# Identity products that nobody reads, and another order of the first chunk's steps, in a fused mLSTM and GELU kernel

## The chip, the cores and the metric

The kernel runs on one core of a Trainium2 chip. The metric is the device time of one execution in microseconds (us). The core's engines work side by side, each through its own list of instructions in the order in which the program issued them: PE (TensorE, matrix products), DVE (VectorE, elementwise work), ACT (ScalarE, functions from tables and copies), POOL (GpSimd) and the queue that issues the transfers. A step that needs another engine's result waits on a semaphore.

## What is computed

An mLSTM cell runs over 768 positions for 4 batches of 8 heads of 40 elements. Its output, as 3072 rows of 320, goes through a layer with an exact GELU.

```python
# per position t; q, k, v, o: (B, H, D), i and f: (B, H); B, H, D = 4, 8, 40
m_new = maximum(f + m, i)
C = exp(f + m - m_new) * C + exp(i - m_new) * outer(v, k)
n = exp(f + m - m_new) * n + exp(i - m_new) * k
y = sigmoid(o) * (C @ q) / maximum(abs(n @ q), 1)
# then x = y as (3072, 320), w_in (320, 2048), w_out (2048, 320)
h = x @ w_in
out = (0.5 * h * (1 + erf(h / sqrt(2)))) @ w_out
```

The two weights come as 64-bit floats.

## The kernel before

The sequence is cut into six chunks of 128 positions, and each chunk into its four batches. For a chunk the cell becomes a handful of matrix products; the layer follows for the 512 rows of the chunk. The chunks after the first are computed in one dense pattern, in which the cell of the next chunk runs between the rows of the layer of this one. The first part, called the front, has more to do: it computes the gates, the cell of chunk 0, the cell of chunk 1, the layer of chunk 0, and it converts the weights from 64-bit to 32-bit floats on DVE and ACT, piece by piece.

The front is played from a list of words. A letter names a step, a digit its batch or piece:

```python
FRONT = """
    O0 L0 P0 g0 L2 E t0 P1 N P2 w0 K L1 D w1 Q P3 O2 s0 w2 t1 O1 c0 J v0 K t2 s1 L3 w3 g1 v1 O3 J y0 c1 K B5 y1 s2
    x0 O4 L4 t3 J x1 K B4 g2 L5 s3 v2 c2 g3 c3 y2 v3 G0 x2 J K A M1 y3 x3 L6 J M0 K H K O5 O7 J T0 J W0 O6 A S0 W1 K
    ...
"""
def play(order, steps):
    for word in order.split():
        if word[0] not in "AU":
            first_up()
        steps[word[0]](*[int(x) for x in word[1:].split(",") if x])
```

Small letters are steps of chunk 0 and capitals the same of chunk 1: m mask, w weights, g gate, t turn (transpose k and q), s scores, c carry (the state), v values, y finish, x turn y. E and N are the later gates, D and Q their transposed decays. L and O load q, k and v, o; P fetches a piece of the weights, B loads maxima; K and J are the two halves of a conversion, Z sums of weights; A and U are up-products (x times w_in, then GELU), F down-rows (times w_out).

The steps that the change touches, with cuts. The class is `Cell`, `c` the chunk and `b` the batch. Line numbers in the profile are those of this kernel: L360 is the transpose in `turn`, L381 the product in `scores`, L399 and L404 those in `carry`, L428 in `values`, L453 in `turn_y`; L521 and L527 are the up-products, L634 the down-rows of chunk 0.

```python
def weights(self, b):            # w: exp(a - M), from a broadcast M
    ...
            if h % 4 == 0:       # chunk 0 only
                pm = ps_mm.tile([P, 4, L], F32, name="pm", tag="b")
                for j in range(4):
                    nc.tensor.matmul(pm[:, j, :], row[...].to_broadcast([3 * BH, P]), M_parts, ...)
                nc.tensor.matmul(pm, eye, beyond..., ...)
    ...
def turn(self, b):               # t
    for src, store, name in ((kb, self.kT, "kT"), (qb, self.qT, "qT")):
        pt = ps_tr.tile([P, NP, L], F32, name="pt", tag="tr")
        for p in range(NP):
            nc.tensor.transpose(pt[:, p, :], src[n % NLD][...], ident)
        store[b] = two.tile([P, NP, L], F32, name=name, tag=name)
        nc.scalar.copy(out=store[b], in_=pt)
...
def scores(self, b):             # s
    ps = [pool.tile([P, NP, L], F32, name="ps", tag=tag) for hip in range(2)]
    for p in range(NP):
        for hip in range(2):
            r = halves[hip]
            nc.tensor.matmul(ps[hip][:, p, :], kT[r, p, :], qT[r, p, :], start=True, stop=True)
    for hip in range(2):
        nc.vector.tensor_tensor(out=w, in0=ps[hip], in1=w, op=OP.mult)      # w: half of W[n]

def carry(self, b):              # c
    pf = ps_h.tile([P, H + NP, D1], F32, name="pf", tag="h")
    pc = pf[:, H:H + NP, :]
    if c == 0:
        self.weigh_values(b)     # vw = v * exp(...), on DVE
    ...
            nc.tensor.matmul(pc[halves[hip], p, :], kb[n % NLD][...], vw[...], start=True, stop=True)
    ...
            if c == 0:
                nc.scalar.copy(out=st, in_=pc[r])
    ...
def values(self, b):             # v
    ph = pool.tile([P, H, D1], F32, name="ph", tag=tag)
    for h in range(H):
        for r in halves:
            nc.tensor.matmul(ph[r, h, :], Pm[:, h, r], vb[n % NLD][:, h, :], start=True, stop=True)
    ...
def turn_y(self, b):             # x
    ...
    for k in range(NX + 1):
        nc.tensor.transpose(px[:, k, :], ob[n % NLD][:, k * P:(k + 1) * P], ident)
    nc.scalar.copy(out=xT[:, :, t], in_=px)
```

`finish` (y) is six instructions on DVE, the first three of which read the result of `values`. `conv_one` (K) is an instruction on DVE, two on ACT that follow it, and two more on DVE; `conv_two` (J) is two on DVE, the first of which needs ACT's, and then the fetch of a later piece.

Of the kernel before, what the change touches and what calls it, by code (L numbers as in the profile page):

```python
# [15 lines left out]
P = 128  # L16
# [6 lines left out]


FRONT = """
    O0 L0 P0 g0 L2 E t0 P1 N P2 w0 K L1 D w1 Q P3 O2 s0 w2 t1 O1 c0 J v0 K t2 s1 L3 w3 g1 v1 O3 J y0 c1 K B5 y1 s2
    x0 O4 L4 t3 J x1 K B4 g2 L5 s3 v2 c2 g3 c3 y2 v3 G0 x2 J K A M1 y3 x3 L6 J M0 K H K O5 O7 J T0 J W0 O6 A S0 W1 K
    M2 J C0 T1 U U K K Z V0 J T2 L7 G1 A M3 W2 J W3 S1 C1 Z A K S2 K Z Y0 C2 J G2 J V1 T3 K K U U Y1 S3 Z C3 J V2 K
    J F F F K J K J Z Z K J K J F F G3 J K K X0 V3 F J F Z F F F J K J Y2 K K J X1 K F F J K J J F Z F X2 F B9 B8 Y3
    X3 F"""  # L30
DOWN = """
    M0 Z M1 T0 W0 F F T1 W1 Z G3 Z F S0 Z S1 C0 M2 Z C1 G1 G0 M3 V0 Y0 Z V1 W2 Z F F T2 W3 F T3 F G2 Z Y1 S2 S3 C2
    V2 C3 Y2 V3 F F Y3 X0 F F X1 X2 F F X3 F"""
# [3 lines left out]
def kernel(  # L37
# [16 lines left out]
    nc = tc.nc  # L54

    B, H, S, D = q.shape
    L = P
    NCH = S // L
# [36 lines left out]
    ident = const.tile([P, P], F32, name="ident")  # L95
# [114 lines left out]
    def decays_turned(e0, e1, g0, g1):  # L210
        e, g = slice(e0, e1), slice(g0, g1)
        gates_turned((ew[:, e], ewT[:, e]), (gg[:, g], gT[:, g]))
        pd = ps_tr.tile([P, g1 - g0, BH], F32, name="pd", tag="tr")
        nc.tensor.matmul(pd.rearrange("p c n -> p (c n)"), last, gT[:, g].rearrange("p c n -> p (c n)"),
                         start=True, stop=True)
        nc.vector.tensor_copy(out=dec[:, g], in_=pd)
# [88 lines left out]

    halves = (slice(0, R), slice(R, P))

    def per_head(t, c, b):
        return t[:, c, b * H:(b + 1) * H].unsqueeze(2)

    class Cell:
# [14 lines left out]
        def weights(self, b):  # L326

            n = self.c * B + b
            W[n] = wts.tile([P, H, L], F32, name="W", tag="W")
            if self.c > 0:  # L330
                M_n = Mb.pop(n)
            for h in range(H):
                r = b * H + h
                if self.c > 0:
                    src = M_n[:, h, :]
                else:


                    if h % 4 == 0:
                        pm = ps_mm.tile([P, 4, L], F32, name="pm", tag="b")  # L340
                        for j in range(4):
                            nc.tensor.matmul(pm[:, j, :], row[:, r + j:r + j + 1].to_broadcast([3 * BH, P]), M_parts,
                                             start=(j == 0), stop=False, skip_group_check=True)
                        nc.tensor.matmul(pm, eye, beyond.unsqueeze(1).to_broadcast([P, 4, L]), start=False, stop=True,
                                         skip_group_check=True)
                    src = pm[:, h % 4, :]
                nc.scalar.activation(out=W[n][:, h, :], in_=src, func=AF.Exp, scale=-1.0, bias=aT[:, self.c, r:r + 1])  # L347
            if self.c > 0 and not 2 * B <= n + NM < 2 * B + NM:
                load_M(n + NM)
# [5 lines left out]
        def turn(self, b):  # L355
            n = self.c * B + b
            for src, store, name in ((kb, self.kT, "kT"), (qb, self.qT, "qT")):
                pt = ps_tr.tile([P, NP, L], F32, name="pt", tag="tr")
                for p in range(NP):
                    nc.tensor.transpose(pt[:, p, :], src[n % NLD][:, 2 * p:2 * p + 2, :].rearrange("p h d -> p (h d)"),  # L360
                                        ident)
                store[b] = two.tile([P, NP, L], F32, name=name, tag=name)
                nc.scalar.copy(out=store[b], in_=pt)
            if 0 < self.c < NCH - 1:
                self.weigh_values(b)
# [6 lines left out]
        def scores(self, b):  # L372
            n = self.c * B + b
            kT, qT = self.kT.pop(b), self.qT[b]

            pool, tag = (ps_tr, "tr") if self.c > 0 and b % 2 else (ps_mm, "a")
            ps = [pool.tile([P, NP, L], F32, name="ps", tag=tag) for hip in range(2)]
            for p in range(NP):
                for hip in range(2):
                    r = halves[hip]  # L380
                    nc.tensor.matmul(ps[hip][:, p, :], kT[r, p, :], qT[r, p, :], start=True, stop=True)  # L381
            for hip in range(2):
                w = W[n].rearrange("p (m two) t -> p m two t", two=2)[:, :, hip, :]
                nc.vector.tensor_tensor(out=w, in0=ps[hip], in1=w, op=OP.mult)  # L384

        def carry(self, b):

            c, n = self.c, self.c * B + b
            qT = self.qT.pop(b)

            pf = ps_h.tile([P, H + NP, D1], F32, name="pf", tag="h")
            pc = pf[:, H:H + NP, :]
            if c == 0:
                self.weigh_values(b)
            if c + 1 < NCH:
                vw = self.vw.pop(b)
                for p in range(NP):
                    for hip in range(2):
                        nc.tensor.matmul(pc[halves[hip], p, :], kb[n % NLD][:, 2 * p + hip, :], vw[:, 2 * p + hip, :],  # L399
                                         start=True, stop=True)  # L400
            if c > 0:
                for p in range(NP):
                    for r in halves:
                        nc.tensor.matmul(pf[r, 2 * p:2 * p + 2, :].rearrange("p h d -> p (h d)"), qT[:, p, r],  # L404
                                         state[b][:, p, :], start=True, stop=True)
                self.far[b] = two.tile([P, H, D1], F32, name="far", tag="far")
                nc.vector.tensor_tensor(out=self.far[b], in0=pf[:, 0:H, :],
                                        in1=per_head(gT, c - 1, b).to_broadcast([P, H, D1]), op=OP.mult)
            if c + 1 < NCH:
                for hip in range(2):  # L410
                    r, m = halves[hip], slice(D1 * hip, D1 * hip + D1)
                    st = state[b][r, :, m]
                    if c == 0:
                        nc.scalar.copy(out=st, in_=pc[r])
                    else:
                        d = dec[r, c - 1, b * H:(b + 1) * H].rearrange("p (m two) -> p m two", two=2)[:, :, hip:hip + 1]
                        self.engine.tensor_tensor(out=st, in0=st, in1=d.to_broadcast([DP, NP, D1]), op=OP.mult)  # L417
                        nc.vector.tensor_tensor(out=st, in0=st, in1=pc[r], op=OP.add)

        def values(self, b):  # L420
            n = self.c * B + b
            Pm = W.pop(n)

            pool, tag = (ps_mm, "a") if self.c > 1 else (ps_h, "h")
            ph = pool.tile([P, H, D1], F32, name="ph", tag=tag)
            for h in range(H):
                for r in halves:
                    nc.tensor.matmul(ph[r, h, :], Pm[:, h, r], vb[n % NLD][:, h, :], start=True, stop=True)  # L428
            if self.c == 0:
                self.hs[b] = ph  # L430
                return
            hs = self.hs[b] = two.tile([P, H, D1], F32, name="hs", tag="hs")
            nc.vector.tensor_tensor(out=hs, in0=ph, in1=self.far.pop(b), op=OP.add)
# [12 lines left out]
        def turn_y(self, b):  # L446
            n, t = self.c * B + b, slice(b * L, (b + 1) * L)
            if self.c > 0:
                px = ps_tr.tile([P, NX + 1, L], F32, name="px", tag="tr")
            else:  # L450
                px = ps_mm.tile([P, NX + 1, L], F32, name="px", tag="b")
            for k in range(NX + 1):
                nc.tensor.transpose(px[:, k, :], ob[n % NLD][:, k * P:(k + 1) * P], ident)  # L453
            nc.scalar.copy(out=xT[:, :, t], in_=px)  # L454
            if self.c > 0:
                load(n + NLD)
            if self.c > 0 and b == B - 1:
                sum_x()
# [259 lines left out]
    def cell_steps(c, letters):  # L718
# [4 lines left out]
    first_g = Hidden(False)  # L723
    n_pieces = range(len(pieces))
    steps = dict(P=fetch, L=lambda n: load(n, 0, 2), O=lambda n: load(n, 2, 4), B=load_M, E=second_gates, N=later_gates,
                 D=lambda: decays_turned(0, 2, 0, 1), Q=lambda: decays_turned(2, NCH - 1, 1, NCH - 1),
                 A=in_turn(first_up_steps(0)), U=in_turn(first_up_steps(1)), F=in_turn(first_down_steps(first_g)),
                 K=in_turn(lambda i=i: conv_one(i) for i in n_pieces), H=sums_begin,
                 J=in_turn(lambda i=i: conv_two(i) for i in n_pieces), Z=in_turn(lambda i=i: in_sum(i) for i in range(8)))
# [46 lines left out]
```

## Time and profile before

| what | value |
|---|---|
| device time, median of 3 | 525.6 us (524.04 to 525.65) |
| span of the profiled execution | 523.9 us |
| PE busy | 503.9 us, 96% |
| DVE busy | 342.0 us, 65% |
| ACT busy | 257.7 us, 49% |
| POOL busy | 60.2 us, 11% |
| moved by DMA | 41.62 MB, mean 79 GB/s |

"Busy" is the time in which an engine has an instruction under way; for PE it does not tell how fast the instruction runs. The granted clock tells that in part: 1.00 is full speed, 0.50 half. A row of the order of time gives the start, the busy time, and in brackets how long the engine was idle before it and whose result ended that. PE instructions of one group overlap a little, so the sum of a group's durations is more than the time it takes.

### The profile page before, as it was taken

How to read it: one execution, taken by the hardware profiler on the slowest of the kernel's cores; microseconds unless marked ns; L12 is line 12 of the kernel's file. 1: busy time of each engine (PE TensorE's matmuls, PEld its weight loads, DVE VectorE, ACT ScalarE, POOL GpSimd, SP SyncE). 2: the span in 40 equal slices, each digit the busy share in tenths (PEclk: the TensorE clock that was granted, in tenths of full speed). 3: DMA queues.
4: the chain of work that ended last, by engine and by line, in shares of the span. 5: the costliest groups of instructions: out<-in, count | busy, mean ns of one | idle time of the engine just before them, and what ended most of it. 6: DMA issues, size and time to landing. Idle time of an engine off the chain costs nothing.

```text
span 523.9 us, 10898 instructions
## 1 busy us (share of the span) xinstructions
PE 503.9 (96%) x4436; PEld 447.9 (85%) x4436; DVE 342.0 (65%) x711; ACT 257.7 (49%) x524; POOL 60.2 (11%) x98
## 2 busy tenths in 40 slices
PE   3778999999999999999999999999999999999997
PEld 2667888877788999988999988999988999988997
DVE  7579669999757898357478356578356547256521
ACT  5785999764342980143881134682134583134200
POOL 3001010000200044000054000053100021000000
PEclk9988999999999999999999999999999999999999
DMA  9989823259900134900124920024940020000001
GB/s 171 166 192 196 210 78 78 73 147 202 199 15 1 60 103 66 178 10 1 41 89 76 167 47 0 27 98 79 155 61 0 1 82 3 26 25 2 1 0 51
DMA packets 111442, 41.62 MB, mean 79 GB/s; under 512 B 101184, under 2 KB 104416, under 8 KB 111392
## 3 DMA queue, kind: packets, MB, share of 16 engines
q1 hardware_dynamic: 111392, 40.92, 37.7%
q8 instruction: 35, 0.57, 0.4%
q14 instruction: 15, 0.12, 0.1%
HBM read 36.90 MB, written 4.01 MB: 78 GB/s over the span
## 4 chain that ended last, share of the span: by engine, by line
PE 93%; DVE 4%; ACT 2%; issue 0%; DMA 0%; DVEq 0%; ACTq 0%
PE po L657 29%; PE pu L587 24%; PE pu L612 7%; PE po L634 7%; PE pu L521 5%; PE ps L381 5%; PE ph L428 4%; PE pt L360 4%; PE pf L404 2%; PE pf L399 2%; PE px L453 2%; PE pu L527 1%; DVE W L384 1%; DVE M L194 1%; DMA f_sb<-in_f_gate_dram 0%
## 5 line engine op out<-in xcount | busy, mean ns | idle before, releaser
L657 PE MATMUL po<-w_out,g 128*128 128x160 f32 x640 | 91.5, 299 | 0.0
L657 PEld LDWEIGHTS po<-w_out,g 128*128 128x128 f32 x640 | 88.0, 190 | 0.3 <-issue 0.3
L587 PE MATMUL pu<-xT,w_in 128*128 128x256 f32 x240 | 63.1, 386 | 0.0
L619 DVE TENSOR_TENSOR g<-pu,g 128x512 f32<-128x512 f32 x60 | 39.6, 688 | 34.5 <-PE pu L612 33.8
L587 PEld LDWEIGHTS pu<-xT,w_in 128*128 128x128 f32 x240 | 44.1, 190 | 10.3 <-issue 5.0
L384 DVE TENSOR_TENSOR W<-ps,W 128x512 f32<-128x512 f32 x48 | 30.2, 684 | 31.1 <-ACT W L347 21.1
L454 ACT COPY xT<-px 128x384 f32<-128x384 f32 x24 | 11.1, 479 | 77.8 <-PE px L453 77.8
L347 ACT ACTIVATE W<-Mb,aT 128x128 f32<-128x128 f32 x160 | 48.9, 391 | 0.1
L620 ACT ACTIVATE g<-g 128x512 f32<-128x512 f32 x60 | 37.1, 630 | 22.1 <-DVE g L619 20.2
L657 PE MATMUL po<-w_sums,sums 128*128 128x160 f32 x320 | 47.3, 302 | 0.0
L617 ACT ACTIVATE g<-pu 128x512 f32<-128x512 f32 x20 | 11.9, 597 | 70.0 <-PE pu L612 70.0
L657 PEld LDWEIGHTS po<-w_sums,sums 128*128 128x128 f32 x320 | 44.0, 190 | 0.4
L323 POOL TENSOR_SCALAR_AFFINE_SELECT Mb<-Mb 128x1024 f32<-128x1024 f32 x20 | 22.3, 1123 | 189.8 <-DMA Mb<-M_d 189.6
L612 PE MATMUL pu<-xT,w_rest 64*128 64x256 f32 x320 | 40.0, 389 | 0.0
L670 DVE TENSOR_TENSOR o_sb<-po,o_sb 128x320 f32<-128x320 f32 (+1 forms) x27 | 12.5, 464 | 41.5 <-PE po L657 36.2
L587 PE MATMUL pu<-x_sums,in_sums 128*128 128x256 f32 x160 | 37.8, 379 | 0.0
L612 PEld LDWEIGHTS pu<-xT,w_rest 64*128 64x128 f32 x320 | 29.3, 186 | 9.3 <-issue 6.6
L634 PE MATMUL po<-w_out,g 128*128 128x320 f32 x128 | 35.5, 434 | 0.0
L587 PEld LDWEIGHTS pu<-x_sums,in_sums 128*128 128x128 f32 x160 | 30.4, 190 | 4.1
L634 PEld LDWEIGHTS po<-w_out,g 128*128 128x128 f32 x128 | 23.9, 190 | 9.4
L521 PE MATMUL pu<-xT,w_in 128*128 128x256 f32 x128 | 29.3, 385 | 0.5 <-DVE W L384 0.5
L417 POOL TENSOR_TENSOR state<-state,dec 64x164 f32<-64x164 f32 x24 | 11.1, 464 | 162.0 <-PE pf L404 158.2
(132 smaller groups left out, 872.2 us busy)
## 6 DMA issues: line engine op xcount, KB each, us to landing
Mb<-M_d SPq DMA_DIRECT2D x20, 512.0 KB, 3.9
bits<-in_moe_w_in_dram SPq DMA_DIRECT2D x20, 256.0 KB, 3.9
bits<-in_moe_w_out_dram SPq DMA_DIRECT2D x16, 320.0 KB, 3.3
vb<-in_v_dram SPq DMA_DIRECT2D x24, 160.0 KB, 4.7
ob<-in_o_gate_dram SPq DMA_DIRECT2D x24, 160.0 KB, 4.0
qb<-in_q_dram SPq DMA_DIRECT2D x24, 160.0 KB, 4.6
kb<-in_k_dram SPq DMA_DIRECT2D x24, 160.0 KB, 4.7
out_dram<-o_sb SPq DMA_DIRECT2D x24, 160.0 KB, 2.9
```

Source lines behind the costliest of these rows:

```text
L323: nc.gpsimd.affine_select(out=t, in_=t, compare_op=OP.is_ge, fill=1.0e30, base=0, pattern=[[0, H], [1, L]], channel_multiplier=-1)
L347: nc.scalar.activation(out=W[n][:, h, :], in_=src, func=AF.Exp, scale=-1.0, bias=aT[:, self.c, r:r + 1])
L360: nc.tensor.transpose(pt[:, p, :], src[n % NLD][:, 2 * p:2 * p + 2, :].rearrange("p h d -> p (h d)"), ident)
L381: nc.tensor.matmul(ps[hip][:, p, :], kT[r, p, :], qT[r, p, :], start=True, stop=True)
L384: nc.vector.tensor_tensor(out=w, in0=ps[hip], in1=w, op=OP.mult)
L521: nc.tensor.matmul(banks[-1][e][:, i - i0, :], w_in[:, x, e, i * P:(i + 1) * P], xT[:, x, t0:t1], start=(x == 0 and i == i0), stop=False, ...
L587: nc.tensor.matmul(to[:, j, :], lhs[:, (f0 + j) * P:(f0 + j + 1) * P], rhs, start=(first and j == 0), stop=(last and j == 1), skip_group_c ...
L612: nc.tensor.matmul(pair[e][:, j, :], w_rest[halves[e], (f0 + j) * P:(f0 + j + 1) * P], xT[halves[e], NX, HT * h:HT * (h + 1)], start=False ...
L619: nc.vector.tensor_tensor(out=blk[e][h], in0=x, in1=y, op=OP.add)
L620: nc.scalar.activation(out=blk[e][h], in_=blk[e][h], func=AF.Gelu)
L634: nc.tensor.matmul(po[b], g.t[:, f, b * L:(b + 1) * L], w_out[:, f, :], start=(f == 0), stop=(f == NF - 1))
L657: nc.tensor.matmul(bank[at][:, i, :], lhs(j, t), rhs(j), start=(first and i == 0 and j == 0), stop=(i == n - 1 and j == HF - 1), skip_grou ...
```

## The change

A step `I` sets a counter. Each of six places in which PE begins a tile of results reads the counter and issues that many products of the identity with itself into the tile, before the products that the step needs; these overwrite what the identity products left, so that nobody reads it. The counter is then zero. The purpose is in the name `keep_clock`: to give PE something to do where it would stand idle, so that its clock stays up. Besides, the words of the front stand in another order; the later parts have the order of before.

```diff
 FRONT = """
-    O0 L0 P0 g0 L2 E t0 P1 N P2 w0 K L1 D w1 Q P3 O2 s0 w2 t1 O1 c0 J v0 K t2 s1 L3 w3 g1 v1 O3 J y0 c1 K B5 y1 s2
-    x0 O4 L4 t3 J x1 K B4 g2 L5 s3 v2 c2 g3 c3 y2 v3 G0 x2 J K A M1 y3 x3 L6 J M0 K H K O5 O7 J T0 J W0 O6 A S0 W1 K
-    M2 J C0 T1 U U K K Z V0 J T2 L7 G1 A M3 W2 J W3 S1 C1 Z A K S2 K Z Y0 C2 J G2 J V1 T3 K K U U Y1 S3 Z C3 J V2 K
-    J F F F K J K J Z Z K J K J F F G3 J K K X0 V3 F J F Z F F F J K J Y2 K K J X1 K F F J K J J F Z F X2 F B9 B8 Y3
-    X3 F"""
+    O0 L0 P0 I3 g0 L2 P1 E I2 t0 N w0 L1 K P2 D w1 Q O2 s0 P3 w2 t1 O1 c0 J v0 K t2 s1 w3 L3 g1 v1 I3 O3 J y0 c1 K
+    B5 y1 s2 x0 O4 t3 L4 J x1 K B4 L5 g3 s3 I7 v2 g2 c2 c3 y2 G0 v3 x2 K J A L6 y3 M1 J x3 M0 K H K O7 O5 J T0 J W0
+    O6 A S0 K W1 M2 J C0 T1 U U K K Z V0 J T2 L7 A M3 W2 J G1 S1 C1 Z W3 A K K G2 S2 Y0 C2 Z J J K V1 T3 G3 K U U Y1
+    S3 Z C3 J V2 K F F F J Z K J J K K J Z K J F F J V3 K X0 K F J Z F J F F F K J K Y2 K J X1 K F F F J K J F J F Z
+    X2 B8 B9 Y3 X3 F"""
...
+    idle = [0]
+
+    def keep_clock(steps):
+
+        idle[0] = steps
+
+    def unread(bank):
+        for _ in range(idle[0]):
+            nc.tensor.matmul(bank, ident, ident, start=True, stop=True, skip_group_check=True)
+        idle[0] = 0
...
                 pt = ps_tr.tile([P, NP, L], F32, name="pt", tag="tr")
+                unread(pt[:, 0, :])
...
             pf = ps_h.tile([P, H + NP, D1], F32, name="pf", tag="h")
             pc = pf[:, H:H + NP, :]
+            unread(pf.rearrange("p h d -> p (h d)")[:, 0:P])
...
             ph = pool.tile([P, H, D1], F32, name="ph", tag=tag)
+            unread(ph.rearrange("p h d -> p (h d)")[:, 0:P])
```

The same call stands in `weights`, `scores` and `turn_y`, and `I=keep_clock` joins the table of steps.

More of the change, by code (lines that the diff above doesn't have):

```diff
@@ L340, in weights @@
                         pm = ps_mm.tile([P, 4, L], F32, name="pm", tag="b")
+                        unread(pm[:, 0, :])
                         for j in range(4):
@@ L377, in scores @@
             ps = [pool.tile([P, NP, L], F32, name="ps", tag=tag) for hip in range(2)]
+            unread(ps[0][:, 0, :])
             for p in range(NP):
@@ L451, in turn_y @@
                 px = ps_mm.tile([P, NX + 1, L], F32, name="px", tag="b")
+            unread(px[:, 0, :])
             for k in range(NX + 1):
@@ L725 @@
     steps = dict(P=fetch, L=lambda n: load(n, 0, 2), O=lambda n: load(n, 2, 4), B=load_M, E=second_gates, N=later_gates,
-                 D=lambda: decays_turned(0, 2, 0, 1), Q=lambda: decays_turned(2, NCH - 1, 1, NCH - 1),
+                 I=keep_clock, D=lambda: decays_turned(0, 2, 0, 1), Q=lambda: decays_turned(2, NCH - 1, 1, NCH - 1),
                  A=in_turn(first_up_steps(0)), U=in_turn(first_up_steps(1)), F=in_turn(first_down_steps(first_g)),
```

## The prediction

> **What bounds the kernel now.** I read the page first, for the engine that is full; then the busy time by stage, for where it is not; then the granted clock in windows of 3.41 us; then the order of time on PE, ACT and DVE around the places so found.
>
> The page, busy time of the engines and the forty slices of the span:
>
> ```profile
> PE 503.9 (96%) x4436; PEld 447.9 (85%) x4436; DVE 342.0 (65%) x711; ACT 257.7 (49%) x524; POOL 60.2 (11%) x98
> ...
> PEclk9988999999999999999999999999999999999999
> ```
>
> TensorE (PE) is busy for 96% of the span, and the clock dips only in slices 3 and 4 (26 to 52 us). Then the stages, cut where one limit gives way to another (columns: stretch and length in us, then busy us and instructions of PE, of its weight loads, DVE, ACT, POOL, then granted clock, DMA share, GB/s):
>
> ```profile
> 0.00:16.00 16.00, 5.50 (x27) 3.90 (x27) 13.05 (x39) 9.22 (x20) 4.56 (x26) 1.00 0.83 166
> 16.00:29.19 13.19, 12.79 (x130) 10.44 (x131) 5.39 (x12) 10.05 (x30) 0.00 (x0) 1.00 1.00 173
> 29.19:54.60 25.41, 19.98 (x241) 17.19 (x240) 24.55 (x56) 17.16 (x36) 2.66 (x2) 0.87 0.97 195
> 54.60:62.30 7.70, 7.25 (x80) 6.06 (x78) 3.84 (x7) 7.59 (x16) 0.00 (x0) 1.00 0.96 217
> 62.30:137.70 75.40, 75.40 (x572) 59.72 (x573) 65.38 (x165) 55.63 (x102) 2.34 (x2) 1.00 0.53 123
> ```
>
> To 16 us DVE computes the gates (13.05 of 16); to 29 PE is the fuller; from 29.19 to 54.6 DVE never waits and PE has 5.4 us of holes; then ACT (7.59 of 7.70); from 62.3 on PE is full, and the table of waits has none of PE after 62.3. So every us by which the dense stretch starts sooner is a us of the total, and a us inside the DVE-bound stretch is worth nothing unless PE itself set the pace there.
>
> The clock in 29.19 to 54.6, same columns:
>
> ```profile
> 31.65:35.06 3.41, 1.03 (x22) 1.02 (x24) 3.24 (x11) 1.96 (x3) 0.00 (x0) 1.00 0.98 224
> 35.06:38.47 3.41, 3.41 (x25) 3.19 (x22) 3.27 (x10) 2.89 (x6) 0.18 (x1) 0.50 0.66 193
> 38.47:41.88 3.41, 2.82 (x54) 2.34 (x52) 3.34 (x6) 2.42 (x5) 1.21 (x1) 1.00 0.95 152
> 41.88:45.29 3.41, 1.25 (x36) 1.13 (x36) 3.27 (x11) 1.61 (x5) 0.00 (x0) 1.00 0.92 286
> 45.29:48.70 3.41, 3.41 (x42) 3.15 (x39) 3.34 (x6) 1.83 (x5) 1.27 (x1) 0.50 1.11 205
> ```
>
> Twice a window in which PE was busy for about a third (1.03 and 1.25 us of 3.41) is followed by one at half clock. And PE in order of time at the second (start us, us, then what; brackets: idle before, and the releaser):
>
> ```profile
> 40.51 1.13 PE L428 MATMUL ph<-vb,W 128*64 128x41 f32 x32
> 43.29 0.67 PE L399 MATMUL pf<-vw,kb 128*64 128x41 f32 x16 [1.65 <-DVE vw L369]
> 44.71 0.67 PE L399 MATMUL pf<-vw,kb 128*64 128x41 f32 x16 [0.75 <-ACT state L414]
> 45.20 1.86 PE L428 MATMUL ph<-vb,W 128*64 128x41 f32 x32
> 46.99 0.90 PE L453 MATMUL px<-ident,ob 128*128 128x128 f32 x3
> 47.69 4.11 PE L521 MATMUL pu<-xT,w_in 128*128 128x256 f32 x16
> ```
>
> From 44.71 PE waits for nobody until 62.30: the slow window lies at the head of the dense stretch, on the path. The first (35.06 to 38.47) lies under a DVE that never waits.
>
> [...] half clock for two stretches of 3.41 us, 10.23 us apart, three such windows. [...] The first stretch is not recorded, but the 16 score products took 2.01 us at 20.4 against 0.89 at 78.0, so PE ran at half speed until about 24.8.
>
> [...] the window from 35.06, mostly transposes by time, was followed by full clock. [...]
>
> **The change, part by part.** *The products.* The order names four numbers: I3, I2, I3, I7. The first is overwritten by the second before any step reads it, so PE gets three groups: 2 at the head of the first turn, 3 at the head of c1, 7 at the head of v2; 12 in all. Nothing is removed. Cost of one: a product of 128 columns in fp32. The score step makes 4 pairs, each pair side by side on the two halves of the array, in 0.89 us: 0.22 us; at half clock 2 x 0.22 = 0.44.
>
> - The 2 before t0: 0.9 us at half clock. PE waits there for k until 7.88, but the group stands behind the gate transpose that ends at about 7.7, so the eight transposes end some 0.7 us later, near 10.5. The next thing PE does starts at 10.65, released by DVE; ACT has no other work from 10.5 to 13.8. Cost 0.
> - The 3 before c1: 0.67 us. PE idles from 31.55 to 34.02 for DVE's vw; bank free at about 32.5, done by 33.2. Cost 0. Its window rises from 1.03 to 1.7 us busy, half full; but whether 35.06 to 38.47 then is fast matters little, as DVE took the scores of s2 at 36.86 and of s3 at 41.55 without waiting.
> - The 7 before v2: 1.54 us. They start at 40.5, v2 runs from 42.05 to 43.2. The vw for c2 is ready at 43.16, and DVE asks for v2's result at 43.56. Cost 0, with 0.1 to 0.3 us to spare. The window 41.88 to 45.29 then holds 0.2 + 1.1 + 0.67 + 0.58 = 2.55 us, 75%, instead of 37%.
>
> *What it brings.* If 45.29 to 48.70 is at full clock, the same work takes: v3 0.91 instead of 1.69 (the chain of waits at 86.9, and at 45.4), px 0.33 instead of 0.83 (at 111.6), the up-products 3.46 instead of 3.91 (at 73.5). 0.78 + 0.50 + 0.45 = 1.73 us, which is 3.41 / 2.
>
> *Does it arrive?* The up-products end at about 51.0 instead of 52.8. ACT waited 1.81 us for them at 52.89 and has its Gelu table at 51.08, so it moves by about 1.7; its later work hangs on two exponents that DVE delivers at 52.1 and 53.5, still in time (52.5 and 53.9). ACT's chain to the masked weights W and so DVE's product, which releases PE at 62.30, comes about 1.5 us sooner. I carry 1.5 to 1.7.
>
> *The order.* Up to 40 us the lists of PE, DVE and ACT are the same as before except for the products; only loads move (the second piece before the gate store, the third and fourth later, k and q of t1 sooner), and PE waited for a load only once, 0.2 us. Later, PE's list differs only in where the down rows lie between other steps. On ACT and DVE more moves. The case that counts:
>
> ```profile
> 64.22 1.28 ACT L347 ACT_TABLE_LOAD   x1
> 65.52 2.45 ACT L347 ACTIVATE W<-Mb,aT 128x128 f32<-128x128 f32 x8
> ...
> 69.36 0.69 DVE L297 SCALAR_TENSOR_TENSOR pow<-bits,pow 128x512 uint32<-128x512 uint32 x1 [5.12 <-ACT pow L286]
> ```
>
> DVE waits 5.12 us because a conversion's two ACT steps stand behind that table load and weights; the new order puts them ahead, worth up to 1.28 + 2.45 = 3.7 us to DVE. Two of ACT's table loads fall away as well (37 to 35 in its list). None of this shortens PE, which is full; but it matters: from 69.36 to 135.28 DVE idles only 0.79 + 0.46 us, and its last copy of y3 ends at 135.28, just when PE takes the last turn (135.41). Were PE 1.6 us faster alone, it would wait there. With the new order DVE should be ahead.
>
> Sum: 0 for the products, -1.6 for the clock, 0 for the order: 525.6 - 1.6 = 524.0; a small chance of more (below) makes it **523.9 us**.
>
> **Rivals.** (a) *The clock stays half anyway*, because products in place of a wait do not suffice or the windows fall otherwise: then 525.6, or up to 1.5 us more if the 7 run at half clock (7 x 0.44 = 3.1 us, which delays v2, y2 and so DVE). [...] (b) *DVE or ACT becomes the bound* and eats the gain by 135 us: 525. For: the tie at 135.3. Against: the 3.7 us given to DVE. (c) *The clock also comes up sooner at the start*: with the 2 products the window near 7.8 to 11.2 is about 85% used; if PE then stayed fast, the scores at 20.4 and the mask products behind them would gain 1.1 + 0.7 us or more, and DVE with them: 521 to 522. Against: between 11 and 16 PE waits for DVE, and 2.39 us of idleness at 13.6 to 16 would make it slow again.
>
> **Range and chances.** (a) about 20%, (b) 15%, (c) 10%, the plain sum the rest. The three runs of before spread over 1.6 us (524.04 to 525.65), about what one slow window is worth, so the position of the windows may differ by run. Range 521.8 to 525.4. For 2% the time would have to move 10.5 us; all of PE's half-clock and idle time between 29 and 62 us is 3.4 + 5.9 us, so neither side is likely: faster 0.01, same 0.98, slower 0.01.
>
> **What would show it.** Right: three groups of products, 2, 3 and 7; no half clock after the second hole; v3 near 0.9 us and px 0.33; dense PE from about 60.7; no DVE wait of 5 us near 65; no PE wait near 134. Wrong: half clock again after 45 us; v2 ending after 43.6 with DVE waiting for it; a PE wait on DVE or ACT after 62 that was not there.

## The result, and the profile after

| kernel | device time, median | range | ratio to before, 95% interval |
|---|---|---|---|
| before | 525.56 us (4 executions) | 524.04 to 525.65 | |
| changed | 523.69 us (4 executions) | 523.52 to 523.77 | 0.9971 [0.9953, 0.9989] |

By the medians the change makes the kernel 1.9 us (0.4%) faster: inside the range on record, 0.2 us under the predicted time. The ratios in this text are those on record, which are not ratios of the medians; here the ratio says 0.3%.

The page of the changed kernel, busy time of the engines and the clock in forty slices:

```profile
PE 503.5 (97%) x4460; PEld 448.0 (86%) x4460; DVE 341.2 (65%) x711; ACT 254.7 (49%) x522; POOL 60.1 (12%) x98
...
PEclk9699999999999999999999999999999999999999
```

PE runs 24 instructions more (12 products, two each), ACT two table loads less (3.0 us less busy). The dip of the clock now shows in slice 2, none in slices 3 and 4.

The changed kernel in windows of 3.41 us, cut where its own clock changes (columns: stretch and length in us, busy us and instructions of PE, of its weight loads, DVE, ACT, POOL, then granted clock, DMA share, GB/s):

```profile
31.85:35.26 3.41, 2.12 (x32) 1.91 (x34) 3.24 (x11) 2.02 (x4) 0.00 (x0) 1.00 0.89 229
35.26:38.68 3.42, 2.23 (x24) 1.84 (x22) 3.28 (x10) 3.33 (x8) 1.09 (x1) 1.00 0.92 222
38.68:42.09 3.41, 3.34 (x47) 3.10 (x48) 3.34 (x7) 2.39 (x6) 0.00 (x0) 1.00 1.02 205
42.09:45.50 3.41, 2.63 (x84) 2.40 (x80) 3.24 (x12) 1.31 (x5) 0.00 (x0) 1.00 1.03 258
45.50:48.92 3.42, 3.42 (x27) 3.04 (x24) 3.35 (x6) 3.10 (x6) 1.49 (x1) 1.00 0.26 29
```

Where the kernel before had 1.03 and 1.25 us of busy time, there are now 2.12 and 2.63, and no window at half clock follows. The order of time on PE (start us, us, then what; brackets: idle before, releaser) at the head of the dense stretch:

```profile
39.84 1.83 PE L316 MATMUL ph<-ident 128*128 128x128 f32 x14
41.60 1.13 PE L444 MATMUL ph<-vb,W 128*64 128x41 f32 x32
42.75 0.67 PE L414 MATMUL pf<-vw,kb 128*64 128x41 f32 x16
44.17 0.67 PE L414 MATMUL pf<-vw,kb 128*64 128x41 f32 x16 [0.75 <-ACT state L429]
44.66 1.11 PE L444 MATMUL ph<-vb,W 128*64 128x41 f32 x32
45.70 0.55 PE L470 MATMUL px<-ident,ob 128*128 128x128 f32 x3
...
60.20 7.17 PE L538 MATMUL pu<-xT,w_in 128*128 128x256 f32 x32 [0.46 <-DVE W L398]
```

The seven products fill the hole of 1.65 us. The values of v3 take 1.11 instead of 1.86 us, px 0.55 instead of 0.90, the first up-products 3.62 instead of 4.11. From the second carry (44.17, before 44.71) to the first wait after it (60.20, before 62.30) PE needs 16.0 instead of 17.6 us. So of the 2.1 us by which the profiled executions differ there, 1.56 are clock and 0.54 a carry that starts sooner; the spans differ by 2.2 us (523.9 and 521.7).

### The profile page after: what moved, and what is told of

It reads as the page before. It is cut to its first block, busy times and chain, and to the rows that moved or that the text cites. A ratio compares the mean times of both kernels' runs of the same rounds, so it can differ in the third digit from the quotient of the medians.

```text
span 521.7 us, 10943 instructions
## 1 busy us (share of the span) xinstructions
PE 503.5 (97%) x4460; PEld 448.0 (86%) x4460; DVE 341.2 (65%) x711; ACT 254.7 (49%) x522; POOL 60.1 (12%) x98
## 4 chain that ended last, share of the span: by engine, by line
PE 93%; DVE 3%; ACT 2%; issue 1%; DMA 0%; SPq 0%; DVEq 0%; ACTq 0%
PE po L674 30%; PE pu L604 24%; PE pu L629 7%; PE po L651 7%; PE pu L538 5%; PE ps L395 4%; PE ph L444 4%; PE pt L373 4%; PE pf L419 2%; PE pf L414 2%; PE px L470 1%; PE pu L544 1%; DVE M L194 1%; ACT W L359 0%; DMA i_sb<-in_i_gate_dram 0%
## 5 line engine op out<-in xcount | busy, mean ns | idle before, releaser
L604 PEld LDWEIGHTS pu<-x_sums,in_sums 128*128 128x128 f32 x160 | 30.4, 190 | 4.1
```

Source lines behind the costliest of these rows:

```text
L604: nc.tensor.matmul(to[:, j, :], lhs[:, (f0 + j) * P:(f0 + j + 1) * P], rhs, start=(first and j == 0), stop=(last and j == 1), skip_group_c ...
```

## The experiments

Each experiment is an edit of the changed kernel unless it says otherwise; the runs of one job share the runs of the kernel before.

### The order alone

```diff
-    O0 L0 P0 I3 g0 L2 P1 E I2 t0 N w0 ...   v1 I3 O3 ...   s3 I7 v2 ...
+    O0 L0 P0 g0 L2 P1 E t0 N w0 ...   v1 O3 ...   s3 v2 ...
```

> The new order without any identity product. Theory (the products keep the clock up, worth 1.5 us at 45 to 49 us; the order brings some 0.5 us, because the masks on POOL come 0.96 us sooner and no longer meet an SBUF-only conversion of DVE): half clock again in one window near 35 and one near 45 us, last product before the dense stretch at about 44.2, PE dense from about 61.7 instead of 60.2, 525.1 us. Rival 1 (the order does it all, the products are decoration): 523.7. Rival 2 (the order does nothing): 525.6.

Measured: 525.23 us median of 20 executions, 523.79 to 526.68; before 525.69, median of 35, 523.52 to 527.24; ratio 0.9987 [0.9975, 0.9999]. The median is near the theory's 525.1, and rival 1 falls. Rival 2 falls only if 0.46 us between the medians can be trusted, with ranges of 3 us on both sides and an interval that ends at 0.9999. And the profiled execution was one of 524.03 us with no half clock recorded at all, where I had expected two such windows. Its clock comes up near 25.9 us: the four transposes from 24.89 take 1.06 us, as at half speed, and the carry at 25.88 takes 0.67, as at full speed. Counted on from there in steps of 3.41 us, the length of each half-clock stretch in before (35.06 to 38.47 and 45.29 to 48.70), the windows that hold most of its two holes are

```profile
32.75:36.16 3.41, 1.63 (x32) 1.55 (x32) 3.24 (x11) 1.93 (x4) 0.00 (x0) 1.00 0.84 269
...
39.58:42.99 3.41, 1.88 (x48) 1.63 (x44) 3.38 (x7) 2.16 (x4) 0.00 (x0) 1.00 1.14 221
```

They are 48% and 55% busy, and full clock follows both (the transposes at 36.60 take 0.60 us, v3 at 45.16 takes 1.11). So the same holes cost a slow window in one execution and none in another. The slow stretch does not start at one place (the one at the head of the dense stretch at 45.29 us in before and at 43.69 without the seven, below), so that windows counted back from it divide a hole otherwise; that this is the reason is my estimate from these starts, and is not shown. The kernel before varies as well: among its 35 executions, those with a mean clock of 0.990 took 526.4 to 527.2 us and the best, at 0.997, 523.5. My reading of before from one profile was of a middling execution, not of the rule.

### The products alone

The words of the kernel before, with the three groups of products put in:

```diff
-    ... E t0 P1 ...   v1 O3 J y0 c1 ...   s3 v2 c2 ...
+    ... E I2 t0 P1 ...   v1 I3 O3 J y0 c1 ...   s3 I7 v2 c2 ...
```

> The old order with the same three groups of 2, 3 and 7 products. Theory: no half clock after 25 us, DVE stretch as before, so the dense stretch begins at 44.7 as before but runs at full clock, PE dense from about 60.7, 524.0 to 524.1 us. Rival 1 (the order does it all): 525.6. Rival 3 (DVE ties with PE at 135 us in the old order, so that the gain is given back there): 525.0 or more, with a PE wait near 134 us.

Measured: 523.87 us (523.50 to 524.27, 4 executions), ratio 0.9955 [0.9940, 0.9969]. The products do nearly all of it: 523.87 of them alone, 523.69 with the new order, with overlapping ranges. The theory said "no half clock after 25 us", and that was wrong in the detail: this execution had half clock from 34.8 to 38.2 us, after a window with 57% of busy time. With the seven behind it, that window was not free: the scores of s3 came at 39.22 (38.75 in the changed kernel), so the seven started later and v2 with them. No mask delayed DVE here (the mask is taken up below), so it had the vw of c2 ready at 42.36, while PE was in v2, and then waited for v2 itself:

```profile
42.07 1.13 PE L444 MATMUL ph<-vb,W 128*64 128x41 f32 x32
43.02 0.65 PE L414 MATMUL pf<-vw,kb 128*64 128x41 f32 x16
43.30 0.49 DVE L454 TENSOR_TENSOR ob<-ph,ob 128x320 f32<-128x320 f32 x1 [0.53 <-issue]
```

Both the carry and DVE are 0.5 to 0.6 us later here than they could have been. Rivals 1 and 3 fall. DVE still waited 5.13 us for the late conversion, and PE waited for nobody after 61 us: in the old order too, all of DVE's chain moves with ACT and PE.

### Without the seven; the seven alone

```diff
-    ... s3 I7 v2 ...
+    ... s3 v2 ...
```

> The changed kernel without the 7 products before v2; 2 and 3 stay. Theory: full clock at 35 to 38, half clock at about 45.4 to 48.8, 525.1 to 525.3 us. Rival (the first slow window was the one that cost): 523.7.

Measured: 524.55 us median of 16 executions, 523.54 to 526.29, ratio 0.9987 [0.9974, 1.0001]. The clock of the profiled execution, in its own windows:

```profile
30.04:33.45 3.41, 1.93 (x42) 1.65 (x38) 3.24 (x11) 3.38 (x9) 0.00 (x0) 1.00 1.17 213
33.45:36.86 3.41, 3.41 (x34) 3.11 (x31) 3.24 (x11) 2.03 (x4) 0.51 (x1) 0.50 0.74 226
...
40.28:43.69 3.41, 1.63 (x50) 1.40 (x48) 3.27 (x10) 1.61 (x5) 0.00 (x0) 1.00 0.96 250
43.69:47.10 3.41, 3.41 (x45) 3.19 (x42) 3.34 (x6) 1.63 (x5) 1.12 (x1) 0.50 1.00 201
```

The second slow window is back, as expected, after one with 48% of busy time. But the first is there too, in spite of the three products (57%), and the median lies between the two theories, 0.6 us under what I had put. The wide spread is back as well.

```diff
-    O0 L0 P0 I3 g0 L2 P1 E I2 t0 ...   v1 I3 O3 ...
+    O0 L0 P0 g0 L2 P1 E t0 ...   v1 O3 ...
```

> The changed kernel with the 7 alone, without the 2 before t0 and the 3 before c1. Theory: half clock at about 35.2 to 38.6 but not at 45; the scores of s3 end at about 40.5, the 7 at about 42.0, v2 at 43.1, so DVE waits 0.1 us at most for y2; 523.7 to 523.9 us. Rival (a window kept up at 35 is needed, or the 2 at the start bring something): 524.5 or more.

Measured: 523.67 us (523.50 to 524.14, 4 executions), ratio 0.9953 [0.9936, 0.9970], with half clock from 33.3 to 36.7 us in the profiled execution. In the new order, the seven alone give all of the gain. With the seven in place, the two and the three bring nothing that these runs can see, and the slow first window cost DVE a wait of 0.16 us for the scores of s2. Without the seven they may bring something: the run with them has a median of 524.55 us, the order alone 525.23, with ranges that overlap for the most part. The runs don't settle it.

### Three in place of seven

```diff
-    ... s3 I7 v2 ...
+    ... s3 I3 v2 ...
```

> The changed kernel with 3 instead of 7 products before v2. Theory ([...] 7 bring it to 75 to 80%, 3 to about 60%): half clock at about 45 us in some executions and not in others, median 523.8 to 524.8, highest 525.3 or more. Rival (any product in the hole is enough): 523.5 to 524.0 in every run, as with 7.

Measured: 523.66 us median of 20 executions, but 522.37 to 526.05, ratio 0.9970 [0.9957, 0.9983]. This fits the theory's picture: half clock from 43.6 to 47.0 in the profiled execution, after a window with 59% of busy time, and the median of the changed kernel with a tail of 2.3 us above it; that other executions had no slow window there is inferred from their times. The median is 0.1 us under the expected range, and the best execution is 1.15 us under the changed kernel's best, which I did not expect. Two things in the profile can add to this, though it is of an execution of 524.27 us, and they are not told apart. In it the first carry waits for vw and not for v2, so three products hold up nobody there. And all of PE's list is 0.5 us early from the second gate on (6.89 instead of 7.36 to 7.39), because an early copy of DVE took 0.25 us instead of 0.88; that has nothing to do with the seven.

### The kernel before with one mask less

POOL masks the maxima of chunk 1 as they land, in the profile of before first at 38.29 us and next at 46.99. In that profile one of DVE's conversions took 1.46 us instead of 0.69 beside the first:

```profile
38.05 0.68 DVE L297 SCALAR_TENSOR_TENSOR pow<-bits,pow 128x512 uint32<-128x512 uint32 x1
38.77 1.46 DVE L302 SCALAR_TENSOR_TENSOR w_rest<-sig,pow 128x512 f32<-128x512 f32 x1
...
38.29 1.40 POOL L323 TENSOR_SCALAR_AFFINE_SELECT Mb<-Mb 128x1024 f32<-128x1024 f32 x1 [32.99 <-DMA Mb<-M_d]
```

The mask took 1.40 us there, and 1.09 in the same profile at 65.59, where DVE stands in its wait of 5.12 us. Why the two delay each other is not shown. The product with the scores, which reads PSUM where the conversion's tiles are all in SBUF, was not delayed: its pair took 1.28 us with a mask beside it (from 36.76 in the run with the products alone, the mask at 36.99) and without one (from 36.86 in before). Whether that difference is the reason is not shown either. The prediction did not reckon with such a delay. The edit, on the kernel before, leaves out the first of the two masks (one batch of chunk 1 then sees positions that it must not):

```diff
     def mask(self, b):
         t = Mb[self.c * B + b]
+        if self.c == 1 and b == 1:
+            return
```

> The kernel before, leaving out one of the two masks of chunk 1 that POOL applies near 38 us (so the output of one batch of that chunk is not the reference's). Theory (that mask held up an SBUF-only conversion of DVE by 0.77 us, in a stretch in which DVE sets the pace): the conversion takes 0.69 us everywhere between 36 and 42 us, the dense stretch of PE starts up to 0.7 us sooner, median 0.4 to 0.8 us under that of before. Rival (the 0.5 us that the new order brought come from the loads or from the moved conversion): no difference.

Measured: 524.32 us median of 20 (523.08 to 527.08) beside 525.43 for before in the same job, ratio 0.9982 [0.9969, 0.9996]: 1.1 us by the medians, some 0.9 by the ratio, more than the 0.4 to 0.8 expected. The conversion at 38.96 us took

```profile
38.96 0.69 DVE L302 SCALAR_TENSOR_TENSOR w_rest<-sig,pow 128x512 f32<-128x512 f32 x1
```

and the second carry of PE began at 44.13 instead of 44.71. So the mask did hold DVE up in the stretch where DVE sets the pace. Part of the median may be the clock again, for with vw ready sooner the hole is smaller (0.92 instead of 1.65 us before the first of the two carries) and no slow window followed in the profiled execution. What falls is my expectation that the new order is what moved the mask out of the way: in the run with the products alone the old order had the mask at 36.99 us and delayed no conversion (0.68 and 0.69 us), and in the run with the seven alone the new order had it at 37.44 and lost 0.90 us. What the mask waited for was its transfer (the bracket above), and that let it start at 36.99, 37.44 and 38.29 us in these three profiles.

### More products, earlier: a version that beats both

In the changed kernel's first 28 us, the clock goes up and down once (same columns as above):

```profile
7.95:11.36 3.41, 3.31 (x18) 2.88 (x18) 3.27 (x9) 1.79 (x4) 0.00 (x0) 1.00 1.23 215
11.37:14.78 3.41, 1.42 (x13) 0.81 (x11) 3.27 (x10) 0.94 (x2) 0.00 (x0) 1.00 0.38 116
14.78:18.19 3.41, 2.17 (x12) 1.48 (x12) 1.34 (x5) 3.38 (x11) 0.00 (x0) 0.50 1.05 192
18.19:21.61 3.42, 3.04 (x22) 2.58 (x23) 0.84 (x3) 2.23 (x9) 0.00 (x0) 0.50 1.23 181
21.61:25.02 3.41, 3.41 (x23) 2.71 (x22) 2.45 (x5) 1.58 (x7) 0.00 (x0) 0.50 0.97 225
25.02:28.43 3.41, 3.41 (x67) 3.02 (x67) 1.90 (x4) 3.34 (x9) 0.00 (x0) 1.00 0.53 144
```

The clock on record is 1.00 up to 14.78, but the transposes up to 10.5 us have the durations of half speed (four in 1.06 us, later in 0.60). The two products filled the window to 11.36 (97%), and the clock was up from there, by the durations; the next window was 42% busy, and it fell for three windows, in two of which PE sets the pace. Products that keep PE busy from 4 to 16 us should save that. They go into a bank of their own that is free at that time:

```diff
+    def unread_alone(n):
+        if n:
+            fill = ps_mm.tile([P, 4, L], F32, name="fill", tag="a")
+            for _ in range(n):
+                nc.tensor.matmul(fill[:, 0, :], ident, ident, start=True, stop=True, skip_group_check=True)
...
     def second_gates():
         gates_of(1, 2)
         nc.sync.dma_start(out=M_d[0], in_=M[:, 1])
+        unread_alone(n0)                             # waits for the gates, 4.2 to 7.4 us
         gates_turned((a[:, 1:2], aT[:, 1:2]))
...
     def decays_turned(e0, e1, g0, g1):
+        unread_alone(n1 if e0 == 0 else 0)           # waits for the gates, 12.2 to 13.2 us
         gates_turned((ew[:, e], ewT[:, e]), (gg[:, g], gT[:, g]))
+        unread_alone(n2 if e0 == 0 else 0)           # waits for the decays, 13.5 to 16.0 us
```

With n0, n1, n2 = 0, 0, 10:

> The changed kernel with 10 more products of the identity while PE waits for the decays between 13.5 and 16 us. Theory (the clock that the first products brought up at 11 us falls again at 14.8 only because PE then stands idle): full clock from about 11 us on, at least where the windows lie as in the run of the changed kernel, the scores of s0 take 0.9 to 1.1 us instead of 2.0, DVE's first products come 2 to 3 us sooner, the dense stretch up to 2.5 us sooner; 521.0 to 522.5 us. Rival 1 [...]: half clock from about 15 to 25 us as before and 523.7. Rival 2 (the loads are then the bound): full clock from 11 us, but new waits for transfers, 523 or so.

Measured: 521.73 us (521.11 to 521.98), ratio 0.9925 [0.9896, 0.9953]. Rival 2 falls: there was no new wait for a transfer. The scores of s0 took 1.16 us and PE then kept full speed until 30.4. But in the profiled execution the clock came up only during the ten products themselves, by their durations near 16.8 us; they took 4.0 us and pushed the decays back by 1.4. With 7, 0, 10:

> As early_ten, and with 7 more products before the second gate transpose, in the idle time from 4.2 to 7.4 us. Theory: full clock from 8 to 11 us on wherever the windows lie, so a narrower spread than early_ten, 521.0 to 522.5 us. Rival (at that time the products push the transposes and so the gates back): PE wait for DVE shorter, transposes later, no gain on early_ten.

Measured: 520.79 us (519.90 to 521.74), ratio 0.9909 [0.9877, 0.9940]. That is under the expected range, and 0.9 us under the run before, with four overlapping executions each, so the rival is not refuted: the two profiled executions have the same span to 0.1 us. The spread became wider, 1.8 us instead of 0.9, against the theory. In its profile the ten again came at half clock, 13.5 to 16.9, after a window with 67% of busy time. With 7, 0, 7:

> As early_all, with 7 instead of 10 products in the wait for the decays. In early_all's profile the 10 ran at half clock (4.0 us) and held back the decays product from 16.0 to 17.4 us. Theory: 7 end at about 15.1 us at full clock and 16.4 at half, so at most 0.4 us late; 519.8 to 520.8 us, with less spread than early_all (519.9 to 521.7). Rival [...]: half clock to about 24 us in some executions, 522 or more there.

Measured: 521.87 us median of 14 (521.20 to 525.21), ratio 0.9940 [0.9923, 0.9958]. The theory fell and the rival is nearer: with fewer products behind the same hole the median is 1.1 us above that with ten (of which there are only four executions), and one execution lost 3 us. In the profile the window from 10.02 to 13.43 was 63% busy, and half clock followed. With 7, 3, 6:

> As early_7_7, with 3 products in the hole of 1.0 us before the first decays transpose (12.2 to 13.2 us) and 6 behind it. Theory (the window that fell to half clock in early_all was 67% busy, 10.1 to 13.5 us, and that hole is what it lacked): no half clock from 8 us to 30 us, 519.8 to 520.3 us and the narrowest spread. Rival (the 3 run at half clock where the clock is not up yet and delay the transposes): 520.5 or more.

Measured: 520.54 us (520.12 to 521.29, 4 executions), ratio 0.9907 [0.9887, 0.9926]: 5 us under before, 3 under the changed kernel, and 1.3 under 7, 0, 7. The median is 0.2 us above the expected range, where the rival had put it, though the three products ran at full clock in the profile (0.83 us). Nor is the spread of 1.2 us the narrowest, and 7, 0, 10 is too near (520.79) to be told apart. The order of time on PE:

```profile
11.54 0.83 PE L182 MATMUL fill<-ident 128*128 128x128 f32 x6
12.30 0.30 PE L190 MATMUL pg<-ident,ew 32*128 32x32 f32 x2
12.98 0.24 PE L190 MATMUL pg<-ident,gg 32*128 32x32 f32 x1 [0.37 <-DVE aT L191]
13.15 1.60 PE L182 MATMUL fill<-ident 128*128 128x128 f32 x12
15.67 0.41 PE L222 MATMUL pd<-gT,last 128*128 128x32 f32 x2 [0.92 <-DVE gT L191]
...
18.65 1.16 PE L404 MATMUL ps<-qT,kT 64*128 64x128 f32 x16
...
41.07 0.67 PE L423 MATMUL pf<-vw,kb 128*64 128x41 f32 x16 [0.75 <-ACT state L438]
```

No half clock follows the small hole before the decays here, as it did in the profiles of the two runs before. That the three products are the reason fits, but the windows lie at other moments in this execution, and it is not shown. The scores start at 18.65 instead of 20.35 and take half as long, and the second carry comes at 41.07 instead of 44.17: 3.1 us, which is the gain on the changed kernel. Some 0.35 of it is there before the clock has a say: the decays come at 15.67 instead of 16.02, as an early copy of DVE took 0.50 us instead of 0.88. By the durations PE is at full speed from about 7.3 to 30.9 us.

## Why the prediction was right

**"If 45.29 to 48.70 is at full clock, the same work takes" 1.73 us less; "I carry 1.5 to 1.7".** Right: 1.56 us between the second carry and the wait at 60.20. The chain of arrivals is there as worked out: the up-products end at 50.8 (predicted 51.0), PE is dense from 60.20 (60.7).

**"Cost 0" for the 2, the 3 and the 7.** Right in the profile of the changed kernel, where the first window was at full clock, v2 ended at 42.73 and DVE took its result at 43.03: the slack was as thin as said. But it was luck that there was any. It had been read from a profile in which a mask held DVE up by 0.77 us and so hid the cost. In the run with the products alone no mask did, and the first window was slow besides; v2 ended at 43.20, as put on record, and DVE waited 0.53 us for it. It waited so in three of the seven profiles with the seven products (0.25 to 0.56 us). "Matters little" for the first window was wrong with the seven behind it. The seven took 1.76 us (39.84 to 41.60), not 1.54; a product of 128 columns is 0.25 us, not 0.22.

**"The window [...] then holds [...] 75%".** It held 2.63 us, 77%. What I had not seen is that the slow stretch after the hole need not start where it did in that profile (45.29 us; 43.69 without the seven), or come at all (the order alone). The one profile of before gave "3.41 / 2" as the worth of the products; over executions it must be an average, since before itself spreads from 523.52 to 527.24 us. That the profiled execution (525.68 us) lay at the later median (525.69) was luck, and the closeness of predicted and measured time owes something to it.

**"0 for the order".** If a term of the sum was mis-sized, it is this one, and by little: the order alone took the median from 525.69 to 525.23 (ratio 0.9987 [0.9975, 0.9999]); with the products it can't be told from zero. The 0.54 us by which the carry came sooner in the profile goes back to a mask on POOL that hardly met a conversion on DVE (0.80 us instead of 0.68, against 1.46 instead of 0.69 in before); that the order causes this was not shown, and two runs speak against it. Whether the order brings 0.5 us, and by what, stays open.

**"DVE should be ahead"; the tie at 135.3.** The wait of 5.12 us shrank, by the steps given, in the order of time on DVE of the changed kernel:

```profile
63.51 0.69 DVE L297 SCALAR_TENSOR_TENSOR pow<-bits,pow 128x512 uint32<-128x512 uint32 x1 [1.37 <-ACT pow L286]
```

That is 3.75 us (predicted up to 3.7). But it was not needed: with the products alone the wait stayed at 5.13 us and nothing was given back at 135 us. Rival (b) had no ground, for what held DVE in that chain was ACT, which moved along.

**Rival (c)** came true in its first half and failed in its second, as the text had it: clock up from 11.4, down at 14.8. That half clock is recorded there, with the scores at 2.08 us, also supports the reading that PE ran at half speed up to 25 us in before, where the record shows none and the scores take the same 2.08.

## What to carry to other kernels

Where PE has holes ahead of a dense stretch, look at the clock in windows and not only at the hole: products that nobody reads can be free in a wait, and here they were worth 1.9 us in one place and 3 more in others. They are free only as long as the wait lasts: when another delay falls away, or the group itself runs at half clock, it holds up what follows (0.53 us behind the seven, 1.4 behind the ten). And where the slow stretch starts elsewhere in another profile (45.29 us in before, 43.69 without the seven, 43.54 with three) or does not come (the order alone), judge by the range of many executions, not by one profile: the seven did not lower the best time of before (523.0 to 523.5), they took away its tail up to 527.3. The twelve executions of the changed kernel, of the products alone and of the seven alone lie within 523.50 to 524.27.

## What the runs showed that was not expected

The clock fell after windows in which PE was busy for up to 67%, and the share of busy time alone does not decide it. In the first 55 us of these profiles, windows at full clock by the durations that were 27 to 42% busy were all followed by half clock, and windows of 68% and more never. Between 48 and 67% it goes either way: 48, 57 and 67% were followed by half clock in some runs, while 48 and 55% kept the clock in the run of the order alone (above). And 62% kept it in the changed kernel (31.85 to 35.26, above), but not in the run with ten early products:

```profile
27.01:30.42 3.41, 2.13 (x40) 1.62 (x39) 3.27 (x9) 3.39 (x11) 0.00 (x0) 1.00 1.31 188
30.42:33.83 3.41, 3.41 (x34) 3.11 (x35) 3.24 (x11) 2.04 (x5) 0.00 (x0) 0.50 1.03 253
```

The weight-load time differs (1.91 us and 1.62); whether that counts is not shown. To bring the clock up took more, and there the kind of work may matter: 89% of busy time in small products (18.19 to 21.61) did not do it, 97% with identity products and transposes did in the changed kernel (7.95 to 11.36), 89% with identity products did with 7, 3, 6 (3.62 to 7.04; the two products behind it took 0.71 us, 1.22 in the changed kernel), and in the run with ten early products 97% with gate transposes and bf16 products (9.94 to 13.35) did not, as the ten behind it took 4.02 us.
